# A new issue order for the first eight chunks of a linear-attention and feed-forward kernel, with the weight transfers sent back to back

## Chip, core, metric

The kernel runs on one core of a Trainium2 chip. The metric is the time of one execution on the device in microseconds (us); a lower one is better. Every time below is of an execution in the state that the measurement calls fast, if nothing else is said. A trace has its own clock: its span runs from the first to the last instruction and is about 2 us shorter than the time.

## The reference, cut to what matters

```python
# B, H, S, D = 4, 8, 768, 48; d_model 384, d_ff 2048
for t in range(S):
    state = alpha[:, :, t, :, None] * state + einsum('bhd,bhe->bhde', k[:, :, t], v[:, :, t])
    y[:, :, t] = einsum('bhd,bhde->bhe', q[:, :, t], state)
x = y.transpose(0, 2, 1, 3).reshape(B * S, H * D)      # 3072 x 384
h = x @ w_in
return (h * cos(h)) @ w_out
```

The recurrence is computed in 24 chunks of 128 positions. A pair of chunks gives 256 rows of x, and these then go through the feed-forward part.

## The kernel before

The whole program is a list of units. A letter names the kind, a number the chunk, the pair or the part. The list is run through once; each unit appends its instructions to the queue of its engine, so the list fixes the order on every engine, and nothing else reorders it.

```python
ORDER = """
a0 k0 a2 l0 x9 C0 E0 l1 q0 K0 B1 O1 k2 v2 a5 R0 v0 x13 T0 t0 T1 t1 a4 q2 C1 P1 P0 M0 A1 k4 A0 x4
S0 S1 q4 E1 M2 m0 l2 w0 P2 B2 B3 u0 m1 M3 a7 q5 a6 P3 M1 u1 x11 Y1 Y0 C2 y1 y0 R3 R2 T2 t2 k5 a8
...                                            # cut: some 600 more units
"""
```

The kinds that the argument needs:

- SyncE: `a k q v` load a chunk of alpha, k, q or v (for the first four chunks, two at once); `D` transposes by DMA in some later chunks; `o` stores 128 rows of the output.
- GpSimd: `w0 w1` are the two halves of w_in, `w2 w3` those of w_out (they are cast in the transfer). `K` and `R` scale k and q; `B` and `O` do the same on VectorE. `P` casts v, `M` prepares the decay, `b` is a decayed state.
- ScalarE: `l` logarithm of alpha, `E` exponentials, `h` the cosine, `e` evicts a finished output.
- TensorE: `C` cumulative sums, `T` transposes, `S` state, `A` scores, `Y` (or `Q` for a pair) attention output, `H` four blocks of the first feed-forward product, `V` four blocks of the second. `x11` are eleven warm-up matmuls that compute nothing.
- VectorE: `t m u y z g` evict what T, A, S, Y, Q and H left in PSUM, the memory that the matmuls write.

```python
    two = Slots(psum("two", [C, 1024]), 3)      # for C, A, H, Q
    one = Slots(psum("one", [C, 512]), 2)       # for T, S, Y, V
    ...
    def load_w(i):
        n = NF // 2
        if i < 2:
            f = slice(i * n * C, (i + 1) * n * C)
            nc.gpsimd.dma_start(out=w1[:, :, f], ...)          # cut
        ...
    def first(name, i):                         # H: needs w0 for parts 0 and 1, w1 for 2 and 3 of each pair
        ...
    def second(i):                              # V: needs w2 for quarters 0 and 1, w3 for 2 and 3 of each chunk
        ...
    def warmup(n):
        for _ in range(n):
            nc.tensor.matmul((one.free or two.free)[0][:, 0:512], warm[:, 0:C], warm, start=True, stop=True)
```

A warm-up writes into the PSUM buffer that is free next in the list. It waits for whoever still reads that buffer.

## Time and profile before

| | before |
|---|---|
| time, median of 3 | 183.06 us (183.04 to 183.26) |
| span of the traced execution | 181.2 us |
| TensorE idle before 40 us | 5.2 us |
| warm-up matmuls | 37 in the list |
| landing of w0, w1, w2, w3 | 22.29, 29.05, 34.43, 39.83 us |

### The profile page before, as it was taken

Reading aid. Unit: us, or ns where it says so; the run is one execution under the profiler, and the core shown is the slowest. Engines: PE = TensorE matmul, PEld = TensorE weight load, DVE = VectorE, ACT = ScalarE, POOL = GpSimd, SP = SyncE. Lnnn points to the kernel's source line nnn. Section 1 sums busy time; section 2 is a strip of 40 time slices with the busy share of each in tenths; the row PEclk is TensorE's granted clock in tenths of the full one; section 3 lists DMA queues with packets and bytes.
Section 4 is the critical chain, followed back from the end, with each engine's and each line's share of the span. In section 5 each row is a group of like instructions: output and inputs, shape, how many; then the busy total and the mean of one; then the engine's idle time right before and its main releaser. Section 6 shows DMA issues by size and latency. Waiting matters only on the chain.

```text
span 181.2 us, 5257 instructions
## 1 busy us (share of the span) xinstructions
PE 172.7 (95%) x2232; PEld 126.6 (70%) x2233; DVE 126.2 (70%) x155; ACT 110.9 (61%) x124; POOL 77.8 (43%) x130
## 2 busy tenths in 40 slices
PE   7986897999999999999999999999999999999992
PEld 2453686866688588776787876776788767788661
DVE  6358677938789888984889397268787769765530
ACT  3631552597457787978768985978755532446421
POOL 7349880202566045672228309943087714100100
PEclk9999999999999999999999999999999999999999
DMA  5999999989989998989996989999907994001112
GB/s 149 323 285 190 215 214 192 188 139 196 227 179 179 163 224 196 228 147 211 220 211 155 225 187 217 178 202 239 217 7 190 205 162 155 5 0 49 43 43 87
DMA packets 113719, 31.01 MB, mean 171 GB/s; under 512 B 107808, under 2 KB 112928, under 8 KB 113696
## 3 DMA queue, kind: packets, MB, share of 16 engines
q1 hardware_dynamic: 110816, 27.53, 74.0%
q0 software_dynamic: 2880, 3.15, 10.3%
q8 instruction: 17, 0.28, 0.6%
q14 instruction: 6, 0.05, 0.1%
HBM read 25.17 MB, written 4.72 MB: 165 GB/s over the span
## 4 chain that ended last, share of the span: by engine, by line
PE 83%; DMA 8%; POOL 3%; issue 2%; ACT 1%; DVE 1%; POOLq 0%; DVEq 0%
PE one L468 34%; PE two L445 29%; DMA w<-in_moe_w_out_dram 8%; PE two L385 5%; PE one L481 4%; PE two L306 3%; PE two L245 2%; PE one L331 2%; PE one L281 1%; POOL kqb L266 1%; PE two L234 1%; ACT icp L255 1%; PE two L247 1%; POOL kqb L260 1%; PE one L385 1%
## 5 line engine op out<-in xcount | busy, mean ns | idle before, releaser
L458 DVE TENSOR_TENSOR g_sb<-two,c_sb 128x1024 bf16<-128x1024 f32 x48 | 58.0, 1221 | 25.7 <-ACT c_sb L453 25.1
L453 ACT ACTIVATE c_sb<-two,halfpi 128x1024 bf16<-128x1024 f32 x48 | 52.7, 1114 | 33.4 <-PE two L445 32.0
L468 PE MATMUL one<-w,g_sb 128*128 128x384 bf16 x384 | 69.7, 326 | 0.1
L445 PE MATMUL two<-xT,w 128*128 128x256 bf16 x576 | 68.6, 273 | 0.9 <-DMA w<-in_moe_w_in_dram 0.9
L445 PEld LDWEIGHTS <-w 128*128 128x128 bf16 x576 | 55.2, 98 | 9.2 <-DMA w<-in_moe_w_in_dram 1.1
L468 PEld LDWEIGHTS <-g_sb 128*128 128x128 bf16 x384 | 36.0, 98 | 21.5 <-issue 0.4
L336 POOL TENSOR_TENSOR ub<-sc,Em 128x384 bf16<-128x384 f32 x20 | 16.9, 845 | 33.6 <-DVE sc L346 33.4
L260 POOL TENSOR_TENSOR kqb<-k_sb,icp 128x384 bf16<-128x384 f32 x19 | 19.6, 1033 | 20.2 <-DMA k_sb<-in_k_dram 9.3
L270 POOL CAST vpb<-v_sb 128x384 bf16<-128x384 f32 x24 | 12.2, 517 | 33.0 <-DMA v_sb<-in_v_dram 30.5
L311 DVE TENSOR_TENSOR A_sb<-two,mask_f 128x1024 bf16<-128x1024 f32 x20 | 23.5, 1217 | 2.5 <-PE two L306 2.5
L266 POOL TENSOR_TENSOR kqb<-q_sb,cp 128x384 bf16<-128x384 f32 x19 | 19.5, 1033 | 6.2 <-ACT c_sb L453 3.3
L472 ACT ACTIVATE o_sb<-one 128x384 f32<-128x384 f32 x24 | 11.8, 490 | 16.5 <-PE one L468 16.5
L255 ACT ACTIVATE icp<-two 128x768 f32<-128x768 f32 x12 | 9.7, 811 | 14.2 <-PE two L247 9.1
L425 DVE CAST xT<-two 128x768 bf16<-128x768 f32 x10 | 9.6, 956 | 5.9 <-PE two L385 5.9
L346 DVE TENSOR_TENSOR sc<-one,ub 128x384 f32<-128x384 f32 x20 | 11.0, 550 | 3.1 <-PE one L331 3.0
L481 PE MATMUL one<-warm 128*128 128x512 bf16 x36 | 10.3, 442 | 2.9 <-DVE ub L336 1.5
L226 ACT ACTIVATE lnab<-a_sb 128x768 bf16<-128x768 f32 x12 | 10.1, 844 | 2.3 <-DMA a_sb<-in_alpha_dram 2.3
L220 ACT ACT_TABLE_LOAD x8 | 10.3, 1283 | 0.9 <-PEq L510 0.7
L451 ACT ACT_TABLE_LOAD x8 | 10.3, 1283 | 0.1
L256 ACT ACTIVATE cp<-two 128x776 f32<-128x776 f32 x12 | 9.7, 812 | 0.0
L385 PEld LDWEIGHTS <-vpb 128*32 128x32 bf16 (+1 forms) x448 | 8.9, 95 | 1.1 <-issue 0.7
L481 PEld LDWEIGHTS <-warm 128*128 128x128 bf16 x37 | 3.8, 108 | 7.4 <-issue 3.4
(65 smaller groups left out, 128.3 us busy)
## 6 DMA issues: line engine op xcount, KB each, us to landing
out_dram<-o_sb SPq DMA_DIRECT2D x24, 192.0 KB, 2.9
a_sb<-in_alpha_dram SPq DMA_DIRECT2D x20, 192.0 KB, 3.8
k_sb<-in_k_dram SPq DMA_DIRECT2D x20, 192.0 KB, 3.9
q_sb<-in_q_dram SPq DMA_DIRECT2D x20, 192.0 KB, 3.9
v_sb<-in_v_dram SPq DMA_DIRECT2D x20, 192.0 KB, 3.8
w<-in_moe_w_in_dram POOLq DMA_DIRECT2D x2, 768.0 KB, 9.1
w<-in_moe_w_out_dram POOLq DMA_DIRECT2D x2, 768.0 KB, 13.1
a_sb<-in_alpha_dram SPq DMA_DIRECT2D x2, 384.0 KB, 4.1
```

Of the source, the lines that this page charges most:

```text
L260: eng.tensor_tensor(out=kqb[j % 4][:, 0, :, 0:D], in0=slot(k_t, j), in1=icp_t[j // 2 % 3][:, j % 2].rearrange("s (h d) -> s h d", h=H), op ...
L266: eng.tensor_tensor(out=kqb[j % 4][:, 1, :, 0:D], in0=slot(q_t, j), in1=cp.rearrange("s (h d) -> s h d", h=H), op=ALU.mult)
L270: nc.gpsimd.tensor_copy(out=vpb[j % 4][:, :, 0:D], in_=slot(v_t, j))
L311: nc.vector.tensor_tensor(out=A_t[j % 4].rearrange("s (h t) -> s h t", h=H), in0=two[("A", j)].rearrange("s (h t) -> s h t", h=H), in1=(ma ...
L336: eng.tensor_tensor(out=ub[j % 3][:, :, 0:96].rearrange("r p (a e) -> r p a e", a=2), in0=src.rearrange("r p (a e) -> r p a e", a=2), in1= ...
L385: nc.tensor.matmul(t[32 * c : 32 * c + 32, kt * C : (kt + 1) * C], lhsT, rhs, start=start, stop=stop, skip_group_check=True)
L445: nc.tensor.matmul(t[:, m * n : (m + 1) * n], w1[:, kk, f * C : (f + 1) * C], x_t[g % 3][:, kk, bs].rearrange("r b t -> r (b t)"), start=( ...
L453: nc.scalar.activation(out=c_s.take((name, i)), in_=two[(name, i)], func=AF.Sin, bias=halfpi, scale=1.0)
L458: nc.vector.tensor_tensor(out=g_t[g % 3][:, fs, bs], in0=shaped(two[(name, i)], name), in1=shaped(c_s[(name, i)], name), op=ALU.mult)
L468: nc.tensor.matmul(one[("o", j)][:, 0:DM], g_t[j // 2 % 3][:, f, j % 2], w2[:, f], start=(f == 0), stop=(f == NF - 1))
L472: nc.scalar.activation(out=o_s.take(j), in_=one[("o", j)][:, 0:DM], func=AF.Copy)
L481: nc.tensor.matmul((one.free or two.free)[0][:, 0:512], warm[:, 0:C], warm, start=True, stop=True)
```

## The change

Its intent: fill TensorE's early holes, and have the weights in SBUF sooner. Only the first 310 of some 695 units of the list change; by then the feed-forward part has reached the eighth chunk. All code and the rest of the list stay.

```diff
-a0 k0 a2 l0 x9 C0 E0 l1 q0 K0 B1 O1 k2 v2 a5 R0 v0 x13 T0 t0 T1 t1 a4 q2 C1 P1 P0 M0 A1 k4 A0 x4
-S0 S1 q4 E1 M2 m0 l2 w0 P2 B2 B3 u0 m1 M3 a7 q5 a6 P3 M1 u1 x11 Y1 Y0 C2 y1 y0 R3 R2 T2 t2 k5 a8
-v4 E2 b1 S2 u2 w1 T3 S3 K4 t3 b2 A3 M5 w2 M4 R4 A2 m3 H0 H1 m2 u3 T4 t4 h0 g0 w3 Y3 Y2 y2 y3 b3 K5
+a0 l0 x9 C0 E0 q0 k0 a2 O0 O1 B1 l1 v0 v2 a5 x10 C1 K0 P0 P3 M1 k2 x1 T1 a4 E1 q2 T0 t0 t1 x6 A0
+K3 A1 w0 M0 P1 P2 B2 m0 m1 l2 R3 x4 S1 S0 u0 k4 q4 u1 C2 Y1 O2 E2 a7 k5 a6 q5 Y0 y1 x1 T2 w1 y0 w2
+b1 R4 M2 S2 t2 T3 u2 t3 S3 A2 B4 b2 A3 H1 v4 w3 v5 T4 a9 a8 v6 k6 q6 q7 m3 m2 h1 u3 v7 t4 H0 h0 Y3
 ...            (cut: eight further lines of each; the lists are the same again from unit D12 on)
```

Besides the order, warm-ups go from 37 to 31, and some scalings change engine: R0, R2, B3 and K4 become O0, O2, K3 and B4 early on, and B6, O7, O8, O11, B11 become K6, R7, R8, R11, K11 later.

More of the change, by code (lines that the diff above doesn't have):

```diff
@@ L17 @@
 ORDER = """
-a0 k0 a2 l0 x9 C0 E0 l1 q0 K0 B1 O1 k2 v2 a5 R0 v0 x13 T0 t0 T1 t1 a4 q2 C1 P1 P0 M0 A1 k4 A0 x4
-S0 S1 q4 E1 M2 m0 l2 w0 P2 B2 B3 u0 m1 M3 a7 q5 a6 P3 M1 u1 x11 Y1 Y0 C2 y1 y0 R3 R2 T2 t2 k5 a8
-v4 E2 b1 S2 u2 w1 T3 S3 K4 t3 b2 A3 M5 w2 M4 R4 A2 m3 H0 H1 m2 u3 T4 t4 h0 g0 w3 Y3 Y2 y2 y3 b3 K5
-P4 h1 g1 H2 H6 h2 H3 g2 a9 q6 v6 v5 k6 q7 h6 h3 a10 q8 k7 g6 g3 O5 H4 H5 V0 H7 V4 V5 V1 V2 V3 V6
-V7 h5 h4 h7 l3 e0 e1 T5 g7 g5 g4 C3 v7 S4 t5 A4 l4 A5 u4 b4 P5 m4 m5 P6 V8 V9 V12 E3 V10 V11 C4 e2
-E4 Q2 V13 V14 S5 B6 z2 M7 R6 M6 H9 O7 u5 S6 H8 h9 u6 V15 T6 O8 P7 K7 H11 g9 o2 e3 h8 t6 k8 g8 o0
-a11 q9 h11 k9 S7 T7 u7 t7 g11 H10 K8 V20 V16 V17 A6 A7 D8 R9 h10 l5 g10 V21 V22 K9 m7 m6 a12 a13
-D9 C5 E5 V18 V19 Q3 v8 b5 P8 b7 M8 M9 A8 A9 z3 k13 V23 e4 l6 H12 o1 q11 v9 h12 m9 m8 P9 S8 H13 u8
-g12 H14 a15 V24 H15 h13 e5 h14 g13 q10 v10 b8 g14 Q4 z4 C6 S9 V25 h15 E6 V26 g15 o3 k11 k10 H17
-H18 o5 o4 q12 q13 k12 a14 h17 u9 V27 H16 V28 P10 R10 M10 O11 B11 K10 K13 R12 b9 M11 M12 R13 D10
-D11 v11 K12 e6 h18 V29 D13 D12 g17 a16 a17 v12 v14 v13 k15 S10 h16 g18 g16 u10 H19 V30 V31 h19 g19
+a0 l0 x9 C0 E0 q0 k0 a2 O0 O1 B1 l1 v0 v2 a5 x10 C1 K0 P0 P3 M1 k2 x1 T1 a4 E1 q2 T0 t0 t1 x6 A0
+K3 A1 w0 M0 P1 P2 B2 m0 m1 l2 R3 x4 S1 S0 u0 k4 q4 u1 C2 Y1 O2 E2 a7 k5 a6 q5 Y0 y1 x1 T2 w1 y0 w2
+b1 R4 M2 S2 t2 T3 u2 t3 S3 A2 B4 b2 A3 H1 v4 w3 v5 T4 a9 a8 v6 k6 q6 q7 m3 m2 h1 u3 v7 t4 H0 h0 Y3
+Y2 g1 H2 M3 h2 H3 h3 y2 g0 y3 g2 H6 h6 g3 g6 K5 H5 k8 k7 M4 q8 H4 h5 H7 V4 V5 V0 h4 V1 h7 P4 b3 l3
+V2 V3 V6 V7 e0 g5 g4 g7 O5 T5 e1 t5 C3 E3 V8 S4 u4 A4 A5 b4 P5 V9 V10 R6 K6 V11 V12 e2 l4 m5 m4 o2
+o0 Q2 z2 C4 S5 V13 k9 q9 M6 P6 M5 K7 u5 R7 P7 M7 H9 T6 V14 E4 h9 V15 a11 a12 t6 S6 H8 e3 g9 b5 u6
+h8 g8 H11 T7 t7 H10 R8 K8 h11 K9 a10 M9 R9 g11 M8 V16 S7 V17 A7 A6 a13 u7 D8 h10 g10 V20 D9 V21
+k10 V18 V22 m6 m7 l5 C5 E5 l6 V19 Q3 V23 A8 v8 q10 z3 e5 A9 b7 K10 H12 o3 m8 H13 P8 h12 S8 m9 g12
+e4 h13 H14 H15 h14 q13 v9 V24 u8 v10 k13 q12 q11 b8 P9 R10 g13 Q4 g14 R11 C6 S9 V25 z4 u9 o5 H17
+h15 k11 k12 D10 a14 a15 E6 b9 g15 R13 K11 h17 H18 V26 V27 H16 V28 P10 D11 R12 K13 M11 v11 o1 M10
+K12 M12 e6 h18 V29 D13 o4 D12 g17 a16 a17 v12 v14 v13 k15 S10 h16 g18 g16 u10 H19 V30 V31 h19 g19
 V36 V37 e7 V38 l7 V32 A10 A11 P11 b10 m10 V39 C7 m11 e9 P12 E7 l8 V33 S11 Q5 u11 z5 A13 A12 P13 o9
```

## The prediction

> **What bounds the kernel now.** I read the page first (busy shares, slices), then the chain of work that ended last, then the timelines of TensorE and GpSimd for the first 46 us, then the landing of each weight transfer.
>
> The page, busy rows, slices and the chain by line:
>
> ```profile
> span 181.2 us, 5257 instructions
> PE 172.7 (95%) x2232; PEld 126.6 (70%) x2233; DVE 126.2 (70%) x155; ACT 110.9 (61%) x124; POOL 77.8 (43%) x130
> ...
> PE   7986897999999999999999999999999999999992
> ...
> DMA  5999999989989998989996989999907994001112
> ```
>
> One digit is 4.53 us. TensorE is short of 9 in the first seven slices (0 to 31 us) and in the last, nowhere else; the DMA engines are full from the second slice on. So TensorE sets the end, and whatever can be won by order lies in the first 31 us.
>
> Busy time by ten microseconds (columns: window, its length, busy PE, PEld, DVE, ACT, POOL with instructions, granted clock, DMA share, GB/s):
>
> ```profile
> 0.00:10.00 10.00, 8.46 (x46) 3.67 (x46) 4.88 (x28) 4.38 (x5) 5.99 (x22) 1.00 0.90 243
> 10.00:20.00 10.00, 8.12 (x182) 5.38 (x184) 6.62 (x10) 2.25 (x3) 7.37 (x14) 1.00 1.10 224
> 20.00:30.00 10.00, 8.40 (x195) 6.95 (x192) 8.40 (x12) 5.03 (x5) 5.80 (x9) 1.00 1.19 212
> 30.00:40.00 10.00, 9.86 (x83) 7.89 (x81) 5.53 (x6) 7.47 (x7) 1.00 (x1) 1.00 1.13 173
> 40.00:50.00 10.00, 10.00 (x146) 6.75 (x145) 7.96 (x9) 6.50 (x11) 3.86 (x8) 1.00 0.99 201
> ```
>
> The idle time is 1.54 + 1.88 + 1.60 + 0.14 = 5.2 us, and the warm-up matmuls, which compute nothing, are another 10.3 us (36 recorded, the group L481). From 40 us on the units follow each other at constant pitch, start to start: 1.31 us for a first-matmul unit (H), 0.65 for a second one (V). Nothing is left to win there.
>
> The timeline of TensorE, the pieces that end the early holes:
>
> ```profile
> 15.77 2.53 PE L481 MATMUL one<-warm 128*128 128x512 bf16 x11 [1.51 <-DVE ub L336]
> 18.24 0.35 PE L385 MATMUL one<-qkT,ub 128*32 128x128 bf16 x12
> ...
> 23.25 2.79 PE L445 MATMUL two<-xT,w 128*128 128x256 bf16 x24
> ...
> 29.09 6.73 PE L445 MATMUL two<-xT,w 128*128 128x256 bf16 x60 [0.92 <-DMA w<-in_moe_w_in_dram]
> ```
>
> The eleven warm-ups wait for a PSUM buffer that unit u0 frees, then run until 18.3; the output matmuls Y1 behind them start at 18.24. Their last other need, the masked scores m1, ended at 16.9, so 1.4 us are lost there. At 29.09 H2 waits for the second half of w_in.
>
> The chain in order of time (start, length, what):
>
> ```profile
> 25.04 14.78 DMA w<-in_moe_w_out_dram
> 39.87 2.76 PE one L468 x16
> ```
>
> The last weight transfer w3 ends the chain's early part: V2 starts at 39.87, when w3 has landed (39.83). The four transfers are issued by GpSimd at:
>
> ```profile
> 13.87 0.94 POOL L208 DMA_DIRECT2D w<-in_moe_w_in_dram  x1
> ...
> 19.26 0.80 POOL L208 DMA_DIRECT2D w<-in_moe_w_in_dram  x1
> ...
> 22.98 0.94 POOL L212 DMA_DIRECT2D w<-in_moe_w_out_dram  x1
> ...
> 25.04 0.94 POOL L212 DMA_DIRECT2D w<-in_moe_w_out_dram  x1
> ```
>
> and land at 22.29, 29.05, 34.43 and 39.83. In the trace's packets the weight queue is empty between about 21.0 (end of w0's data) and 22.7 (start of w1's); the loads of q, k, v and alpha fill that hole. From w1 to w3 there is no further hole.
>
> **What the Trainium skill says.** "DMA: Bandwidth & Descriptors", section "Issuing engines are not separate DMA queues": transfers issued by different engines share the same 16 DMA engines and interleave. The trace agrees: while w2 and w3 are under way, the issue of one 192 KB v load takes SyncE 7.73 us instead of about 0.7. The same page, "Queues, rings and completion order", says that each engine goes round between its queues packet by packet; here the weight queue moves about 92 KB per half microsecond in large packets, and the load queue beside it 7 to 18. The same page, "Why a DMA increments its semaphore by 16 and not by 1": only all sixteen increments mean landed. That matters here: the middle one of w1's sixteen comes at 27.2, the last at 29.05; for w3 38.1 and 39.83. "TensorE: Matmul & The Clock Gate", "What's actually happening": half rate after an idle window of about 3.4 us. The trace agrees at its start (nine 512-column warm-ups in 4.02 us, later thirteen in 2.97).
>
> **The change, part by part.** No instruction's code changes. Six warm-ups go (37 to 31 in the order, about 6 x 0.213 = 1.3 us, worth nothing where they only fill holes). Some scalings of q and k swap engine (VectorE 0.55 to 1.3 us, GpSimd 1.0 to 1.3). The two orders are the same again from unit D12 on, and on TensorE from V29, which starts at 79.70 before. So the gain is the time by which TensorE arrives there earlier.
>
> *Attention front.* The SyncE order keeps sizes by position, so I give each position its old landing time: k0 6.6, v0 9.1, v2 10.3, k2 12.4, q2 14.8, q4 17.1. C1 no longer stands behind the first transposes: x10 ends near 8.6, the log of alpha 2 near 8.9, so C1 runs 8.95 to 10.2 (10.90 before) and its exponentials end at 11.7 (13.6 before). On VectorE O0, O1, B1 take 8.2 to 10.4, so T1 and T0 run 10.4 to 11.4, and t0, t1 (0.65 each) end at 12.8: 0.8 us later than before. The six warm-ups wait for t0's buffer, so scores A0, A1 run at 13.4 to 14.0. B2, m0, m1 (1.2 each) then end at 16.3 (16.9 before). P1, now behind w0 on GpSimd, ends near 15.3; S1, S0 then finish by 16 and do not hold anything. u0 follows m1, 16.9; Y1 starts at 16.9 instead of 18.24, because x11 is gone: 1.3 us earlier. From there O2 0.55, y1, y0 0.55 each, t2 0.7, u2 0.55, t3 0.7 follow on VectorE: t3 ends near 21.4, scores A2, A3 at 22.1 (23.3 before).
>
> *Weights.* w0 stands behind K3, which needs k2 (12.4) and takes 1.3 us: issued at 13.7, 0.2 earlier than before; landing about 22.1. w1 stands behind M0, P1, P2, R3 (0.2 + 0.5 + 0.5 + 1.0 us): issued near 16.8 and w2 near 17.7 in place of 19.26 and 22.98; w3 behind b2 near 21.4. All are queued before the previous one ends, so the 1.7 us hole closes on the queue as a whole. On the slowest engine, whose increment counts, w0 ended only at 22.29 less latency and its hole was 1 us or so. With the 0.2 us of w0 the last increments come 1.2 to 2 us earlier: w1 near 27.3, w3 near 38.2.
>
> *Together.* H1 starts at 22.1, then T4, H0, Y3, Y2 take 4.9 us (23.25 to 28.18 before): 27.1, and H2 waits for w1 until about 27.3. H2, H3, H6, H5, H4, H7 are 6 x 1.31 = 7.9 us, V4, V5, V0, V1 4 x 0.65 = 2.6: V2 could start at 37.8, and w3 lands at 38.2. So V2 starts at 38.2 in place of 39.87, 1.6 us earlier. The warm-ups and idle time removed before 22 us gain no more than that, since both weights and the VectorE row stand behind them. Behind V2 everything is at the old pitch. 183.06 - 1.6 = 181.4 us.
>
> **Rivals.**
> *The weights stop being the limit.* If the hole closes wholly on the slowest engine too, w1 lands at 26.5 and w3 at 37.5; TensorE's own row then gives V2 at 37.5: gain 2.4, 180.7 us. For it: w1's laggard (29.05 against 27.66 for the next) could be chance.
> *The weights gain nothing.* The DMA engines are full in any case; if the weight queue's share falls because the load queue is always full beside it, or the same laggard persists, w3 lands near 39.3: gain 0.5, 182.5 us. Against it: before, the share was already 90% with loads waiting.
> *The displaced loads become the wait.* The 300 KB that the loads moved in the hole move later. By my count of the load queue's bytes k5 and q5 land by 36 and v4 near 38, v5 near 39; T5 needs the first two near 40.8, S4 needs v4 near 42. A slack of 3 us or more: I expect no wait. If it failed, the gain would be eaten: 183 us. Later in the run slack is smaller but real: before, v8 was in place 2.8 us ahead of S8.
> *The clock.* Fewer warm-ups, but no gap that I work out in the first 22 us is over 1.2 us; a cold stretch would cost a microsecond or two.
>
> **Range and chances.** Gain 1.6, with 0.5 and 2.8 as likely ends: 180.2 to 182.6. The gain is capped: TensorE cannot have H2 before about 26.5 by its own row, 2.6 us, and faster by over 2% needs 3.66. I give it 0.05. Slower by over 2% needs 3.66 us of new waits in a row that has none: 0.02.
>
> **What would show each step.** Right: Y1 starts near 16.9; w1 issued near 17 and no hole in the weight queue near 21; H2 near 27.3 and V2 near 38.2, each just behind the landing of w1 and w3; no TensorE idle time from 40 us to the end; V29 near 78.1. Wrong: H2 or V2 not waiting for weights; a wait of TensorE for v, k or q between 38 and 80; P1 or R3 so late on GpSimd that S1 or w1 slips; slices of the clock below 9.

## More of the kernel before

The prediction shows the page's slices, the busy time by windows, the timeline of TensorE and the weight issues. One more line, the chain of work that ended last, by engine (shares of the span):

```profile
PE 83%; DMA 8%; POOL 3%; issue 2%; ACT 1%; DVE 1%; POOLq 0%; DVEq 0%
```

Read from the last instruction back, TensorE alone carries 83% of the time. The one large piece that is not on an engine is the DMA part, 8%: the weights.

## The result, and the profile after

| | before | after |
|---|---|---|
| time, median of 4 | 183.05 us (182.88 to 183.26) | 181.53 us (181.43 to 182.12) |
| span of the traced execution | 181.20 | 179.66 |
| landing of w0, w1, w2, w3 | 22.29, 29.05, 34.43, 39.83 | 22.02, 27.09, 32.23, 37.52 |
| start of Y1, H2, V2, V29 | 18.24, 29.09, 39.87, 79.70 | 17.26, 27.27, 37.75, 77.69 |
| last unit of TensorE, V91 | 177.02 | 175.00 |
| last landing to end of span | 0.97 | 1.43 |

The ratio is 0.9923, with a 95% interval from 0.9900 to 0.9946. It is the mean time of one kernel's fast runs over that of the other's of the same rounds, so not quite the ratio of the medians. The change is within 2%, and faster beyond the noise.

The page of the changed kernel, the lines that answer to those of before:

```profile
span 179.7 us, 5249 instructions
...
PE   7978799999999999999999999999999999999991
...
DMA  5999999989999998699998989999719993010112
...
PE 91%; DVE 4%; issue 1%; ACT 1%; DVEq 0%
```

Of the first seven slices of TensorE four are below 9 now, the last of them the fifth; before it was five, the last of them the seventh. In the chain the DMA part is gone: TensorE has 91%, and VectorE, which feeds it in the first 22 us, 4%.

Busy time by windows, the same columns as in the prediction:

```profile
0.00:10.00 10.00, 8.80 (x48) 3.90 (x49) 4.71 (x28) 4.38 (x5) 5.26 (x22) 1.00 0.91 246
10.00:20.00 10.00, 7.93 (x193) 5.52 (x192) 7.80 (x13) 5.17 (x6) 8.43 (x13) 1.00 1.16 231
20.00:30.00 10.00, 9.32 (x196) 7.90 (x194) 8.82 (x13) 3.34 (x3) 2.00 (x4) 1.00 1.19 193
30.00:40.00 10.00, 10.00 (x79) 7.51 (x78) 7.85 (x7) 8.19 (x8) 2.03 (x4) 1.00 1.10 178
```

Idle time before 40 us fell from 5.2 to 1.20 + 2.07 + 0.68 = 3.95 us. The rest of the gain lies in warm-ups that no longer take TensorE's time: their group was busy for 10.3 us before and is for 9.1 now.

The timeline of TensorE:

```profile
12.46 1.46 PE L481 MATMUL one<-warm 128*128 128x512 bf16 x6 [0.78 <-DVE qkT L286]
...
17.26 0.35 PE L385 MATMUL one<-qkT,ub 128*32 128x128 bf16 x12 [0.56 <-DVE ub L336]
...
22.42 1.48 PE L445 MATMUL two<-xT,w 128*128 128x256 bf16 x12
...
27.27 8.04 PE L445 MATMUL two<-xT,w 128*128 128x256 bf16 x72
35.15 5.36 PE L468 MATMUL one<-w,g_sb 128*128 128x384 bf16 x32
```

Y1 (17.26) waits for u0 and no longer for warm-ups. H1 starts at 22.42, H2 at 27.27, and neither has a wait before it. From 27.27 on the work is continuous: 72 matmuls of H, then 32 of V. The weight issues:

```profile
13.35 0.93 POOL L208 DMA_DIRECT2D w<-in_moe_w_in_dram  x1
...
16.30 0.80 POOL L208 DMA_DIRECT2D w<-in_moe_w_in_dram  x1
17.10 0.92 POOL L212 DMA_DIRECT2D w<-in_moe_w_out_dram  x1
...
21.79 0.94 POOL L212 DMA_DIRECT2D w<-in_moe_w_out_dram  x1
```

In the packets of the trace the weight queue moves at least 70 KB in every half microsecond from 17.0 us to 28. Before, it moved 50 KB in all between 21.0 and 22.5: the hole is closed. (KB is 1024 bytes here.)

So TensorE's row is 2.12 us ahead at V2, 2.01 us ahead from V29 to the last unit, and the span is 1.54 us shorter. The missing 0.46 lie after the last landing, in the program's end: there GpSimd's second drain starts 0.34 us after the instruction before it, where it was 0.04 before, and takes 0.17 us in place of 0.04.

### The profile page after: what moved, and what is told of

Read it like the earlier page. It is cut to its first block, busy times and chain, and to the rows that moved or that the text cites. A ratio compares the mean times of both kernels' runs of the same rounds, so it can differ in the third digit from the quotient of the medians.

```text
span 179.7 us, 5249 instructions
## 1 busy us (share of the span) xinstructions
PE 171.9 (96%) x2225; PEld 126.0 (70%) x2227; DVE 121.7 (68%) x152; ACT 111.6 (62%) x124; POOL 78.8 (44%) x133
## 4 chain that ended last, share of the span: by engine, by line
PE 91%; DVE 4%; issue 1%; ACT 1%; DVEq 0%
PE one L468 36%; PE two L445 35%; PE two L385 5%; PE one L481 3%; PE two L306 3%; PE one L281 2%; PE one L331 2%; PE two L245 2%; DVE kqb L266 1%; DVE qkT L286 1%; PE one L385 1%; PE two L247 1%; PE two L234 1%; PE two L300 1%; ACT icp L255 0%
## 5 line engine op out<-in xcount | busy, mean ns | idle before, releaser
L445 PE MATMUL two<-xT,w 128*128 128x256 bf16 x576 | 68.3, 273 | 0.0
L445 PEld LDWEIGHTS <-w 128*128 128x128 bf16 x576 | 55.2, 98 | 8.1
L468 PEld LDWEIGHTS <-g_sb 128*128 128x128 bf16 x384 | 35.9, 98 | 20.9
L260 POOL TENSOR_TENSOR kqb<-k_sb,icp 128x384 bf16<-128x384 f32 x21 | 21.0, 1000 | 23.4 <-DMA k_sb<-in_k_dram 11.0
L481 PE MATMUL one<-warm 128*128 128x512 bf16 x29 | 9.1, 462 | 2.5 <-DVE warm L106 1.2
L220 ACT ACT_TABLE_LOAD x8 | 10.3, 1283 | 0.9 <-PEq L510 0.7
L451 ACT ACT_TABLE_LOAD x8 | 10.3, 1283 | 0.1
L286 DVE COPY qkT<-one 128x1024 bf16<-128x1024 bf16 x9 | 6.1, 687 | 5.8 <-PE one L281 3.5
```

What stands on the lines that cost most here:

```text
L260: eng.tensor_tensor(out=kqb[j % 4][:, 0, :, 0:D], in0=slot(k_t, j), in1=icp_t[j // 2 % 3][:, j % 2].rearrange("s (h d) -> s h d", h=H), op ...
L445: nc.tensor.matmul(t[:, m * n : (m + 1) * n], w1[:, kk, f * C : (f + 1) * C], x_t[g % 3][:, kk, bs].rearrange("r b t -> r (b t)"), start=( ...
L468: nc.tensor.matmul(one[("o", j)][:, 0:DM], g_t[j // 2 % 3][:, f, j % 2], w2[:, f], start=(f == 0), stop=(f == NF - 1))
```

## The experiments

The timings were made in three groups. Each group ran on one chip with before in the same rounds; on these chips before took 181.9 to 183.7 us. The line numbers of most kernels made for this are four lower (L441 is L445), because their list is printed on fewer lines. All results were correct.

One thing decides how to read the times. In some executions the granted TensorE clock falls to half for one, two or three stretches of 3.41 us each, somewhere in the first 37 us. Before was never affected: its 34 executions in these groups all had a mean clock of 0.997 or more. Of the other kernels, e1, e5 and e13 kept their clock in all six executions, the rest lost it in some or all. The state is still called fast. A mean clock of 0.991 or less in the table marks such an execution.

| run | median (range) of 6 | ratio to before, 95% | mean clocks | H2, V2 in the trace |
|---|---|---|---|---|
| e1_weights_only | 181.90 (181.61 to 182.78) | 0.9965 (0.9930 to 0.9999) | all 0.997 or more | 28.23, 38.74 |
| e2_no_x11 | 182.51 (182.18 to 184.27) | 1.0014 (0.9969 to 1.0060) | 2 of 6 low | 30.42, 40.90 (low) |
| e3_both | 182.81 (182.54 to 184.51) | 1.0033 (0.9989 to 1.0076) | 6 of 6 low | 28.93, 39.41 (low) |
| e4_after_late_weights | 182.78 (182.31 to 184.19) | 1.0023 (0.9984 to 1.0063) | 2 of 6 low | 28.39, 40.52 (low) |
| e5_late_scalings_back | 183.55 (182.71 to 184.81) | 1.0051 (1.0018 to 1.0083) | all 0.997 or more | 27.50, 37.98 |
| e6_both_warm | 182.62 (181.78 to 183.37) | 0.9989 (0.9963 to 1.0015) | 4 of 6 low | 29.05, 39.52 (low) |
| e7_front | 182.25 (182.00 to 189.83) | 0.9965 (0.9945 to 0.9985) | 6 of 6 low, 2 of them slow | 34.32, 46.17 (slow) |
| e8_x6_to_x2 | 181.46 (181.18 to 183.39) | 0.9958 (0.9916 to 1.0000) | 2 of 6 low | 29.22, 39.69 (low) |
| e12_after_again | 181.60 (181.27 to 183.39) | 0.9934 (0.9899 to 0.9968) | 1 of 6 low | 29.26, 39.73 (low) |
| e10_late_t4 | 182.12 (180.76 to 183.19) | 0.9937 (0.9898 to 0.9977) | 3 of 6 low | 27.46, 37.94 (low) |
| e11_late_t4_short_pool | 183.07 (182.00 to 184.54) | 1.0005 (0.9959 to 1.0052) | 2 of 6 low | 26.63, 37.40 |
| e13_front_full | 181.24 (180.73 to 181.49) | 0.9894 (0.9872 to 0.9917) | all 0.997 or more | 26.75, 37.43 |

e1 to e4 were one group, e5 to e8 the second, e12, e10, e11 and e13 the third.

**Weights alone (e1).** The list of before, with two units moved:

```diff
-... R3 R2 T2 t2 k5 a8 v4 E2 b1 S2 u2 w1 T3 S3 K4 t3 b2 A3 M5 w2 M4 R4 ...
+... R3 R2 w1 w2 T2 t2 k5 a8 v4 E2 b1 S2 u2 T3 S3 K4 t3 b2 A3 M5 M4 R4 ...
```

> The order of before, with w1 and w2 alone issued earlier, straight behind the two q scalings (near 18.5 and 19.4 us in place of 19.26 and 22.98). Theory (the gain comes from closing the hole in the weight queue AND from a TensorE front that is there in time; neither suffices): w1 lands near 27.2 in place of 29.05, but the front of before cannot have H2 ahead of the end of Y2, 28.15; V2 near 38.6 in place of 39.87; about 181.8 us, a gain of 1.2. Rival 1 (the weights are all of it): as the changed kernel, 181.5 or less, V2 near 37.8. Rival 2 (the front is all of it, DMA engines are full anyway): w3 lands near 39.8 still and the time is 183.0.

Measured: w1 was issued at 18.59 and landed at 27.86, w3 at 38.70. TensorE's timeline:

```profile
27.67 0.63 PE L381 MATMUL one<-A_sb,vpb 64*32 64x128 bf16 x32
28.23 6.73 PE L441 MATMUL two<-xT,w 128*128 128x256 bf16 x60
```

H2 followed Y2 without a wait (expected 28.15), V2 came at 38.74, just behind w3. TensorE's last unit was at 175.87, 1.15 us ahead of the trace of before; the timed ratio says 0.64 us of 182.8 (between none and 1.3). So earlier weights are worth about half the gain by themselves, and then the front of TensorE limits at H2, as the theory said. Rivals 1 and 2 fall.

But this edit did not close the hole at 21 us. w1's first packets moved near 21.9, some 3.3 us after its issue, when the data of w0 had run out: from 20.5 to 22.5 us the weight queue moved 126 KB, where it moves about 90 in each half microsecond when it is full. What e1 closed is a second hole of before: w2, issued at 22.98, moved its first data at 27.22, and from 26.5 to 28.0 the queue moved 50, 24 and 63 KB.

**The front alone (e2).** `x11` is deleted from the list of before.

> The order of before without the eleven warm-ups that stand ahead of Y1. Theory: Y1 starts near 16.9 in place of 18.24, scores A2 end near 22, but H2 still waits for w1 (29.05) and V2 for w3 (39.83): 183.0 us, no gain over 0.2. Rival 2 (the front is all of it): 181.6 us. Rival 3 (the warm-ups were needed): TensorE at half rate in some stretch before 29 us and a time of 183.5 or more.

Measured: the four executions at full clock took 182.2 to 182.7 us; their median, 182.24, is 0.5 below that of before, within its range. The other two took 184.1 and 184.3. The trace is one of these; the page's row of the granted clock and two rows of the timeline:

```profile
PEclk9998559999999999999999999999999999999999
```

```profile
16.06 0.35 PE L381 MATMUL one<-qkT,ub 128*32 128x128 bf16 x12 [1.51 <-DVE ub L332]
...
24.09 4.26 PE L441 MATMUL two<-xT,w 128*128 128x256 bf16 x24
```

Y1 starts earlier, at 16.06, but from 16.9 to 27.1 us the clock is half, and H0 and H1 take 4.26 us in place of 2.79. So an earlier front alone gains nothing clear, and the eleven warm-ups that looked like pure loss had a use. No trace at full clock was kept, so that H2 then waited for w1, as the theory said, is not shown. Rival 3, which was named only as a chance, came true in two of six.

**Both on the old list (e3 and e6).** e3 has both edits above; e6 keeps five warm-ups (`x5` in place of `x11`).

> Both edits of the two runs above on the order of before, nothing else of the change. Theory: H0 near 22.3 just behind w0, H2 near 27.2, V2 near 37.7, so the whole gain of the change, 181.0 to 181.6 us. If the rest of the change (swapped scalings, C1 ahead of the transposes, loads in another order) matters by itself, this stays over 182.

> The order of before with w1 and w2 early, and five warm-ups ahead of Y1 in place of eleven (none in the earlier run, where the clock fell to half for 7 to 10 us). Theory (both the weights and the front, with the clock kept up): clock 1.0 throughout, Y1 near 17.0, H0 near 22.3, H2 near 27.2, V2 near 37.7: TensorE as early as in the changed kernel, 180.7 to 181.2 us with the short epilogue. If five are too few, the clock falls to half again near 17 us and H2 is no earlier than 28.3.

Measured: e3 lost its clock in all six executions, e6 in four. The trace of e6 has half clock from 22.1 to 25.5:

```profile
22.98 3.99 PE L441 MATMUL two<-xT,w 128*128 128x256 bf16 x24
```

H0 started at 22.98, near the 22.3 expected, then ran slow, and H2 stood at 29.05 again. The two executions of e6 at full clock took 181.78 and 182.25. That is better than before in its own group (182.36 to 183.48) but not the 180.7 to 181.2 expected. So the two edits don't reproduce the change. One reason is the clock. Another is that the hole stayed open, as in e1: in the old order of GpSimd w1 goes out at 18.2, its first packets move near 21.8, and from 20.5 to 22.0 us the weight queue moved 30 KB. So w1 landed at 27.83 and w3 at 38.54; in the changed kernel they landed at 27.09 and 37.52. Two of six executions are too few to put a size on the rest.

**The changed list with late weights (e4).** `w1` moved behind R4, `w2` behind b2, `w3` behind M3.

> The changed kernel with w1, w2 and w3 put back to about their old times (near 19.7, 22 and 23 us in place of 16.3, 17.1 and 21.8). Theory: the hole in the weight queue is back, w1 lands near 29.0 and w3 near 39.5, H2 and V2 wait for them, and of the gain of 1.5 us at most 0.4 stays: 182.7 to 183.1. Rival 2 (the front is all of it): 181.5.

```profile
28.39 9.70 PE L441 MATMUL two<-xT,w 128*128 128x256 bf16 x72 [1.28 <-DMA w<-in_moe_w_in_dram]
```

Measured: TensorE's front was as early as in the changed kernel (H1 at 22.18), but H2 waited 1.28 us for w1, which landed at 28.34. The time was 182.78, that of before. (In this trace the clock was half from 28.4 to 31.9, so V2 is later still than w3; the four executions at full clock took 182.3 to 182.8.) Without early weights nothing of the gain stays. Rival 2 falls.

**The late scalings (e5).** In the changed list K6, R7, R8, R11 and K11 become B6, O7, O8, O11 and B11 at the same places.

> The changed kernel with five scalings of chunks 6, 7, 8 and 11 (B6, O7, O8, O11, B11) given back to VectorE as before, so that GpSimd runs five fewer instructions. Question: TensorE ended 2.01 us earlier in the changed kernel but the span shrank by 1.5, because GpSimd's second drain after the last landing came 0.46 us late (epilogue 1.43 us after the last landing, 0.97 before). Theory A (the epilogue depends on GpSimd's number of instructions): epilogue back to 0.97 and 0.45 us less than the changed kernel, 181.1 where that has 181.5. Theory B (chance of the execution, or of the new order as such): epilogue stays near 1.43. Either way V2 stays near 37.8.

Measured: the end of the program is 0.98 us long again, as theory A expected, but the time rose. The waits of TensorE (total, times, longest):

```profile
PE two L381 <- DVE A_sb L307: 0.9, 1, 0.9
...
PE two L441 <- DVE xT L421: 0.4, 1, 0.4
```

B6 pushed the masked scores of chunks 4 and 5 back, and Q2 waited 0.88 us; a scaling of q on VectorE waited 0.83 us for its load, just ahead of the eviction z4, and a feed-forward unit behind z4 waited 0.41. V2 was at 37.98, 0.23 later than in the changed kernel, V29 1.94 later. So the exchange of engines is a part of the change that works: at the new places these five belong on GpSimd. At other places VectorE might bear them; that was not tried.

**Fewer warm-ups ahead of A0 (e8).** `x6` becomes `x2`.

> The changed kernel with two warm-ups in place of six ahead of A0, which the prediction said these hold up. Theory (weights and TensorE's front now arrive together): A0 near 13.1 in place of 13.84, m0 near 13.9 in place of 14.38, A3 done near 22.1 in place of 22.5, but H1 then meets w0 (22.0), H2 meets w1 (27.1) and V2 meets w3 (37.5): 0.2 us less at most. Rival 1: the front alone is the limit and all 0.5 us are won. Rival 2: the clock falls to half somewhere before 20 us and the time rises by a microsecond or more.

Measured: A0 came earlier as expected (12.43; 13.35 in the trace of the unaltered kernel of the third group), but Y1 stood at 16.89 (16.93 there), because S1 waited for the cast P1 behind w0:

```profile
16.28 0.56 DVE L332 TENSOR_TENSOR ub<-one,Em 128x384 bf16<-128x384 f32 x1 [0.95 <-PE one L321]
```

VectorE, done with the scores, now idles 0.95 us before u0. Four executions took 181.2 to 181.6 us, two 183.4 with half clock. The 0.2 us at most that the theory allowed can't be told from nothing here, and rival 2 came true in two of six.

**The changed kernel a second time (e12).**

> The changed kernel unaltered, on the same chip and in the same rounds as the next two. Runs of before vary by a microsecond on the chips of the earlier experiments (181.9 to 183.7), so this measures the change a second time: ratio to before 0.992 within 0.003, 181.2 to 181.6 us in most runs. If the thinner warm-ups sit at the edge of the clock gate, as a first run at clock 0.987 suggests, one or two of the six runs show a clock below 0.995 and are 0.5 to 2 us longer.

Measured: 0.9934 against 0.9923 the first time. Five executions took 181.3 to 181.9 us. One, the traced one, took 183.39 with this clock row:

```profile
PEclk9999579999999999999999999999999999999999
```

```profile
23.55 2.34 PE L445 MATMUL two<-xT,w 128*128 128x256 bf16 x12
26.18 1.47 PE L445 MATMUL two<-xT,w 128*128 128x256 bf16 x12
```

The first of the two H units ran at half clock, 2.34 us. The same program kept its clock in the first trace. Here it lost 2 us (V2 at 39.73, not 37.75), more than the whole gain. Yet no idle gap of TensorE in this trace is longer than 0.78 us after its first instruction.

**A quicker front with w0 at 12 us (e7, e10, e13).** If weights and front arrive together, both must come earlier to win more. e7 put B1 ahead of O0 and O1, T0 and T1 ahead of C1, and on GpSimd M0, P1, P2 ahead of w0 and K3 behind it:

```diff
-... O0 O1 B1 l1 v0 v2 a5 x10 C1 K0 P0 P3 M1 k2 x1 T1 a4 E1 q2 T0 t0 t1 x6 A0 K3 A1 w0 M0 P1 P2 B2 m0 m1 ...
+... B1 O0 O1 l1 v0 v2 a5 x12 K0 T0 t0 T1 t1 P0 P3 M1 M0 P1 P2 w0 C1 k2 a4 E1 q2 K3 A0 A1 m0 m1 ... B2 ...
```

> The changed kernel with another front: B1 ahead of O0 and O1, the transposes T0, T1 ahead of C1, no warm-ups ahead of A0, and on GpSimd M0, P1, P2 ahead of w0 and K3 behind it, so that w0 goes out at about 12.3 us in place of 13.35. Theory: w0 lands near 21.0, w1 near 26.1, w3 near 36.5; A0 near 11.7, Y1 near 15.1, scores A3 done by 20.7; H1 near 21.1, H2 near 26.1, V2 near 36.6 in place of 37.75: 1.1 us less than the changed kernel, near 180.4. Rival: q4 or k4 are starved by the earlier w0 (landing after 20 us in place of 16.1) and T4 waits; or the clock falls to half since there are fewer warm-ups.

Measured: w0 was issued at 11.91 and landed at 21.41, Y1 started at 15.21. But q4, issued 0.2 us behind w0, landed at 27.19 in place of 16.13, and the transposes of chunk 4 waited:

```profile
PE one L277 <- POOL kqb L262: 5.2, 1, 5.2
```

In this execution the rival came true: from 14.5 to 18.5 us and from 20.0 to 27.5 the load queue moved 16 KB or less in each half microsecond. w3, which stood behind the starved R4 on GpSimd, went out only at 29.36. The trace is of one of the two slow executions (189.8 and 189.4 us). The four fast ones took 182.0 to 182.3, all with a lowered clock, and none was traced, so a wait of 5.2 us is shown for the slow state alone. That a load behind w0 is late in the fast state too is shown by e10, below: there q4 was issued 0.29 us behind w0 and landed at 21.39.

e10 moved what needs q4: `T4 t4` behind V7, `K4 R4` behind w3 (K4 is B4 moved to GpSimd; two more warm-ups stand ahead of y1).

> The quicker front of the earlier run that starved q4, with the need for q4 and k4 moved: T4 and t4 stand behind V7, K4 and R4 on GpSimd behind w3. w0 goes out near 11.9 us, w1 lands near 25.7, w3 near 36.3. Theory (front and weights together set the time, DMA order decides the rest): H1 near 21.4, H2 near 25.8, V2 near 36.3 in place of 37.75, T4 behind V7 adds nothing; TensorE ends 1.0 us earlier than in the changed kernel: 180.3 to 180.6 us where that has 181.4. Rivals: the loads behind q4 (k5, q5, v4) come too late for T5, S4; or the clock falls to half before 22 us.

Measured: the landings were as hoped (w0 20.19, w1 25.86, w3 36.56), but three of six executions lost their clock, and the trace shows a new hole:

```profile
20.22 0.50 PE L321 MATMUL one<-vpb,kqb 64*128 64x96 bf16 x8 [1.31 <-DVE sc L342]
...
21.39 4.46 PE L441 MATMUL two<-xT,w 128*128 128x256 bf16 x24
```

S3 waited for the eviction u2, that for the decayed state b1, and b1 stood behind w1 and w2 on GpSimd. The executions at full clock took 180.8 to 181.8 us.

e13 puts b1 ahead of R3, T4 back behind H0, and `x4` in place of `x3` ahead of C2.

> The quicker front once more, with the hole that put its clock to half closed: on GpSimd the decay b1 stands ahead of R3 (it had waited behind w1 and w2, and u2 and S3 with it, 1.3 us of idle TensorE), T4 is back behind H0, one more warm-up ahead of C2. Theory: S3 near 18.9, scores A3 done near 20.3, H1 near 20.3 just behind w0, H2 near 25.9 just behind w1, V2 near 36.5 just behind w3; clock 1.0 in more of the runs than the three of six before; with the long epilogue 180.2 to 180.8 us in the runs at full clock, a ratio to before near 0.988. Rival: the clock falls to half somewhere all the same in half of the runs, which are then 1 to 2 us longer, and the median is no better than that of the changed kernel.

```profile
26.75 8.04 PE L441 MATMUL two<-xT,w 128*128 128x256 bf16 x72 [1.07 <-DMA w<-in_moe_w_in_dram]
```

Measured: six of six executions at full clock, 181.24 us, ratio 0.9894. H1 started at 20.75, just behind w0 (20.70), then H2 waited 1.07 us for w1 (26.71) and V2 (37.43) for w3 (37.39). So now the weights alone are the limit. w1 and w3 landed 0.8 us later than in e10. A part of that is my own doing: with b1 moved ahead, w1 went out at 17.50, 0.5 us later than in e10. So V2 came at 37.43 rather than 36.5. And the hole in the weight queue is open again: w1's first packets moved near 20.0, and from 18.5 to 20.5 us the queue moved 120 KB. In the changed kernel w1 goes out 4.6 us before the data of w0 has run out (at 20.9), and no hole is left. A w1 issued earlier on this front was tried in e7 alone, where q4 starved. On this chip the changed kernel has the ratio 0.9934. The intervals overlap a little, so e13 is the best version measured, but its lead over the changed kernel (0.4% by the ratios) is not beyond doubt. It lost its clock in none of six executions, the changed kernel in two of ten (one of them in the first measurement, 182.12 us at a mean clock of 0.987).

**The program's end (e11).** e10 with R17, K18, R18, K19, R21 and K22 given to VectorE.

> The same with six scalings of late chunks (17, 18, 19, 21, 22), whose loads land well before their turn, moved from GpSimd to VectorE, so that GpSimd runs fewer instructions. Theory: the epilogue after the last landing shrinks from 1.43 to 0.97 us, and the time by 0.45, to 180.0. Rival: VectorE becomes late there, as it did between 46 and 74 us when chunks 6 to 11 were given back, and the time rises by as much or more.

Measured: the end is 0.97 us, but VectorE was late, as the rival said: TensorE waited 1.09 us at 115.2 for an eviction and 0.62 us at 145.1 for a gate. Another 1.9 us at 16.0 came from the log of alpha 4 (its load landed at 15.03, 13.14 in e10), which has nothing to do with the edit. In all fourteen traces the end after the last landing is 0.96 to 0.98 us when GpSimd runs 128 or 130 counted instructions, and 1.41 to 1.43 when it runs 133 or 134. That is a firm pattern; its cause was not shown.

**What the clock counts.** This is worked out from the kept traces afterwards; no run was made to test it. The granted clock changes only on a grid of windows of 3.41 us, and the grid starts anew in each execution: the first rise to full clock came between 4.4 and 7.1 us in the fourteen traces. Now count TensorE's work in each window in full warm-ups: each matmul counts its columns times the rows and columns of the array that it uses, over 512 x 128 x 128. A window holds about sixteen at most, at 0.216 us each.

- At full clock, the windows after which the clock fell before 40 us held 3.6 (e2), 5.8 (e3), 4.8 (e4), 4.2 (e6), 0 (e7), 5.7 (e8), 4.9 (e10) and 5.7 (e12). Every window after which it stayed held 6.0 or more (in before one warm-up, whose record is missing, is added).
- At half clock, windows with 6.1 or less kept it there, and windows with 6.7 or more ended it.
- Transposes are counted like other matmuls; without them the two groups overlap.

So a busy TensorE can lose its clock: in the window of e12 before the fall (15.10 to 18.52) it was busy for 72% of the time, but much of it with matmuls of `S` and `Y`, which use a half to an eighth of the array. And the chance lies in where the grid starts. In the trace of before no start gives a window under 6.1, and it never lost its clock. In the changed kernel 11% of the starts give one under 6 (the least is 5.7), and it lost its clock in two of ten executions.

## Why the prediction was right, point by point

- **The bound and the cap.** Right. From 27.3 us to the end TensorE runs at its old pitch, and all that was won lies before. One line was misread: TensorE is not short of 9 in the first seven slices but in five of them. (And 22.1 + 4.9 is 27.0, not 27.1. Neither changes the argument.)
- **The hole in the weight queue.** Right, and shown by e4, where late weights take all of the gain away. w1 went out at 16.3 (predicted 16.8) and landed at 27.09 (27.3).
- **The front.** Nearly. Y1 at 17.26 (16.9), H1 at 22.42 (22.1). The step "P1 ... do not hold anything" was right for the changed kernel by a hair only: with the scores earlier (e8), P1 behind w0 held u0, and in the trace of e12 S1 already waited 0.46 us for it.
- **V2.** The step was 38.2, set by w3; it came at 37.75, and w3 landed at 37.52. The mis-sized term is the time won on the slowest DMA engine: I took 1.2 to 2 us off the last increments, and w3 came 2.31 us earlier. So the first rival (the hole closes wholly) was nearer for w3. One reason is that "From w1 to w3 there is no further hole" was misread: before had a second one from 26.5 to 28.0 (see e1), and the 200 KB around it took 1.93 us, in the changed kernel 1.35. So the last step had the wrong side as the limit. Neither H2 nor V2 shows a wait, which the prediction had listed as a sign of being wrong: TensorE's own row was 0.2 us later than the weights both times. The number held because that row came where the sum had it (V2 at 37.75; the sum's own row gave 37.8). That they are balanced is shown from both sides: e4 and e13 have TensorE waiting for weights, e1 has weights that come ahead of TensorE's front at H2.
- **"Behind V2 everything is at the old pitch."** Off by 0.11 us: 2.12 us at V2 became 2.01 at V29.
- **The end of the program** was not in the sum, and cost 0.46 us. So 181.4 against 181.53 owes something to luck: 2.12 - 0.11 - 0.46 = 1.55 where I had 1.6 and no such terms.
- **"The warm-ups ... worth nothing where they only fill holes"**, and the clock rival, argued away by gaps of at most 1.2 us. This step was wrong in kind. The changed kernel kept its clock in eight of ten executions; in the other two it lost a part of the gain (182.12) or all of it (183.39). In e2 and e3, with the warm-ups gone, the clock fell though the longest gap was 1.5 us. Gaps do not separate the cases; the work counted in a window does, as worked out above, and warm-ups add to it.
- **The displaced loads.** Right. v4 landed at 39.00, v5 at 39.67, q5 at 38.22 (36 predicted), and T5 (40.35), S4 (41.97) did not wait. e7 shows what it looks like where a load that is needed soon stands behind the weights.
- **The exchanged scalings** were told only with a cost. e5 showed that the changed kernel needs them where they are.

What stays open: the share of each remaining part of the change (e3 and e6 lost their clock and left the hole open), why GpSimd's end takes longer, and whether the count for the clock holds in kernels other than these.

## What to carry to other kernels

When a large transfer and a compute front meet at the same point, measure both arrival times: moving one alone wins only up to the other, and loads that are needed soon must be issued ahead of the large transfer, since behind it they starve. To send large transfers back to back, issue the next one well before the data of the last runs out: here w1 and w2, where the queue had run empty, moved their first data 2.5 to 4.2 us after their issue. Warm-up matmuls that hold up useful work may still pay by keeping the clock; take them away only with many executions and the granted clock in view. An eviction or a scaling "moved to the idle engine" is free only at a place where nobody waits for that engine.

## What the Trainium skill lacked or had wrong

- "TensorE: Matmul & The Clock Gate", section "Why this matters for your kernels", says to leave no idle gap of TensorE over about 3 us between bursts. That is not enough here: the clock fell to half in an execution of the changed kernel whose longest gap was 0.78 us, and without `x11` with a longest gap of 1.5 us. (Elsewhere the page tells of a kernel whose frequent short idles made the clock swing, but gives no figure for them.) No page gives the amount of work that keeps the clock: in these traces the clock fell after windows of 3.41 us with less work than about six 512-column matmuls of the full array. The lengths of the half-rate stretches (3.41, 6.83 and 10.24 us) agree with the window of about 3.4 us on the same page.
- The same page tells of a variation from run to run for a kernel's first matmuls. It doesn't say that one program can keep its clock throughout one execution and lose it in the midst of the next: the changed kernel kept it in eight of ten, and lost it in two, with 2.0 us of difference at V2 in the traced one.
- "DMA: Bandwidth & Descriptors", section "Queues, rings and completion order", has the engines go round packet by packet, but no number for what a queue of small packets then gets: in the changed kernel mostly 8 to 19 KB per half microsecond beside 66 to 94 KB of the weights. A 192 KB load issued 0.3 us behind w0 took 9.2 us in e10, and one issued 0.2 us behind it took 15 us in the slow execution of e7.
- No page that I found tells of an end of the program that is longer where GpSimd runs more instructions: 0.97 us with 130 or fewer, 1.42 us with 133 or 134. The cause was not shown.
